# Two sequences' result stores moved to GpSimd's DMA queue, and every engine's order planned anew, in a one-core chunk-selected attention and squared-ReLU FFN kernel

## The chip, the cores and the metric

One core of a Trainium2 chip runs one program. The metric is the device time of an execution in microseconds; lower is better. Three runs of the kernel before took 264.72, 265.79 and 266.02 us, median 265.79 us.

## The reference

Four sequences of 768 tokens, 8 heads of 64. Keys are cut into 24 chunks of 32 tokens; for each query an upper bound of its score with each chunk is taken, and only the six best chunks are attended to, under a causal mask. The attention's output, 3072 rows of 512, goes through an FFN of width 2048 with a squared ReLU.

```python
ub = np.sum(np.maximum(q[:, :, :, None, :] * k_min[:, :, None, :, :],
                       q[:, :, :, None, :] * k_max[:, :, None, :, :]), axis=-1)
top_chunks = np.argsort(np.where(causal, ub, -1e9), axis=-1)[..., -top_k:]
scores = np.where(mask, scale * np.matmul(q, k.transpose(0, 1, 3, 2)), -1e9)
x = softmax(scores) @ v                      # 3072 x 512
return (np.maximum(x @ w_in, 0.0) ** 2) @ w_out
```

## The kernel before, in words

A sequence has six tiles of 128 queries. The first tile of each sequence needs no selection (all its chunks are among the six best), so the four first tiles are computed on their own at the start, and their FFN (input `x_first`, 4 tiles) is spread over the first sequence's attention. For the other five tiles of each sequence there are four pairs of heads, 16 pairs in all. Each pair has a **stage A** (`stage_a`): keys and queries are turned (`kT`, `qT`; by TensorE for sequences 0 and 1, by DMA transposes `kt`, `qt` on SP's queue for 2 and 3), VectorE reduces the chunks' largest and smallest keys (`kr`, L697), TensorE makes the bounds (`ub`, L660 and L662), VectorE sorts out the eight largest (`m`, L668), of which the sixth gives the selection (`selb`), which is turned (`sT`) and copied beside the queries (`qsc`) as extra rows, so that the score matmul itself adds the mask. **Stage B** (`stage_b`): scores in banks of 512 columns (`ps`, L782), exp on ScalarE (`e`, L804), the causal mask on VectorE (L759) or GpSimd (L762), values (`av`, L793), and VectorE's division into `x` (L612, L614). When a sequence's four pairs are done, its `x` is turned to `xT` (by TensorE for sequence 0, by five DMA transposes on SP's queue, L389, for 1, 2 and 3), and `ffn` follows: `up` (`ph`, L866), ReLU (`ht`, ScalarE L873 or VectorE L875), square (`h`, VectorE L884), `down` (`py`, L897), a copy to `ob` (L281 on ScalarE, L283 on VectorE), and the store of 256 KB, L910, on SP's queue. The FFN of sequence b is mixed with the attention of sequence b+1; that of the last runs alone at the end.

Nothing of this order is written out. Each piece of work is an `Op` of a `Plan`: the engines that may do it with an assumed cost each, a due time, what it needs, the buffers that it holds, and the DMA packets that it moves. `Plan.order` plays the program through: of the operations that could start on an engine within `wait` of the earliest, it takes the one that is due first, and for work that two engines may do, it takes the engine that could start it first. The instructions are then written in that order, so a due time or a cost that changes can change the order and the engine of all that comes later. Loads (`loads`) go through GpSimd's queue in a fixed sequence, at most eight at once; transposes, stores and the four first raw loads go through SP's queue. Each engine works off its queue in order: an instruction that waits holds up what stands behind it.

While TensorE waits in the first 26 us, `keep_warm` puts matmuls on a constant (`warm`, L539) in the gap, as many as the plan thinks fit (`op.fill`).

Buffers that matter here: `ps` 3, `ff` 2 (for `ph`, `py` and `xt`), `e` 6, `ob` 3. The constants' rows `kqc` for eight (slot, head) pairs are made once and copied seven times at the start (`kq_rows`), by whichever of GpSimd, VectorE and ScalarE the plan picks.

Of the kernel before, what the change touches and what calls it, by code (L numbers as in the profile page):

```python
# [13 lines left out]
ACT = mybir.ActivationFunctionType  # L14
# [66 lines left out]
class Plan:  # L81
# [18 lines left out]
        self.loads = []  # L100

    def op(self, where, due, fn, needs=(), tiles=(), packets=0, turns=False,
           late=0.0):
        op = Op(where, due, fn, [n for n in needs if n is not None],
                [t for t in tiles if t is not None], packets, turns)
        for t in op.tiles:
            t.users.append(op)
        op.late = late
        op.number = -1 if packets and not turns else len(self.ops) - len(self.loads)
        self.ops.append(op)  # L110
        if packets and not turns:
            self.loads.append(op)
        return op

    def order(self):
        free = {e: 0.7 for e in ("PE", "ACT", "DVE", "POOL", "SP")}
        slots = {tag: [(0.0, i) for i in range(n)] for tag, n in self.slots.items()}
        waiting = {}
        count = {}
        for op in self.ops:  # L120
            for t in op.tiles:
                t.left = len(t.users)
            count[op] = len(op.needs)
            for n in op.needs:
                waiting.setdefault(n, []).append(op)
        ready = [op for op in self.ops if not count[op]]
        landed, done = [], []
        dma = Transfers()
        while ready:
            found = []  # L130
            for op in ready:
                if op.packets and not op.turns and op is not self.loads[len(landed)]:
                    continue
                at = 0.0
                new = {}
                for t in op.tiles:
                    if not t.held:
                        new[t.tag] = new.get(t.tag, 0) + 1
                for tag, n in new.items():
                    at = max(at, sorted(slots[tag])[n - 1][0]  # L140
                             if n <= len(slots[tag]) else self.NEVER)
                if at == self.NEVER:
                    continue
                if op.packets and not op.turns and len(landed) >= 8:
                    at = max(at, landed[-8].end)
                for engine, cost in op.where.items():
                    st = max(at, free[engine])
                    for n in op.needs:
                        same = n.engine == engine and not n.packets
                        lag = (0.0 if engine == "PE" else self.BUSY) if same                             else self.HAND_OVER[n.engine]  # L150
                        st = max(st, n.end + lag)
                    for t in op.tiles:
                        if t.psum:
                            for e, end in t.last.items():
                                if e != engine and "PE" not in (e, engine):
                                    st = max(st, end + self.HAND_OVER[e])
                    found.append((st, op, engine, cost))
            assert found, "nothing can start"
            first = min(found, key=lambda f: (f[0], f[1].number))
            st, op, engine, cost = min(  # L160
                (f for f in found if f[2] == first[2] and f[0] <= first[0] + self.wait),
                key=lambda f: (round(f[1].due, 6), f[0], f[1].number))
            ready.remove(op)
            if engine == "PE":
                op.fill = 0
                fresh = [t for t in op.tiles if t.psum]
                if st < self.FILL and fresh and not any(t.held for t in fresh):
                    room = max([free[engine]] + [min(slots[t.tag])[0] for t in fresh])
                    op.fill = max(0, int((st - room - 0.3) / 0.216))
                if st < self.WARM:  # L170
                    cost *= 2
            op.engine, op.start, op.end = engine, st, st + cost
            free[engine] = op.end
            if op.packets:
                dma.add(op)
                if not op.turns:
                    landed.append(op)
            for t in op.tiles:
                if not t.held:
                    t.held = True  # L180
                    slot = min(slots[t.tag])
                    slots[t.tag].remove(slot)
                    t.slot = slot[1]
                t.last[engine] = max(t.last.get(engine, 0.0), op.end)
                t.left -= 1
                if not t.left:
                    slots[t.tag].append(
                        (max(u.end + self.HAND_OVER[u.engine] for u in t.users),
                         t.slot))
            for n in waiting.get(op, ()):  # L190
                count[n] -= 1
                if not count[n]:
                    ready.append(n)
            done.append(op)
        assert len(done) == len(self.ops), "operations left"
        return sorted(done, key=lambda op: op.start)
# [12 lines left out]
def kernel(  # L209
# [9 lines left out]
    nc = tc.nc  # L219
# [17 lines left out]
    QC = 128 * NS  # L237
    VW = 80
    NSET = 4
    P = dict(lead=[0, 207.45, 109.14, 153.29, -29.2, 112.12, 38.49, 53.35, 112.23, 30.95,  # L240
             26.44, 98.99, 127.21, 67.89, -1.38, 124.88], f_due=[452.52,
             -1393.33, -782.42, -326.54], sp='K0 Q0 K1 Q1', rows=[-2963.23,
             -1559.78, 780.78, -565.55, 1811.92, 457.36, -1818.66, -283.78],
# [3 lines left out]
             'q3 v2 v3 k3', shift={}, p0=-2735.84, wait=0.01, xt=(1, 2, 3),  # L247
             sel=2, loads='Q3 K3 V0 V1 Q2 K2 i0 V2 k0 V3 q0 i1 k1 v2 q1 i2 '
             'v0 i3 k2 q2 o1 o0 v1 o2 k3 o3 v3 q3')

    nc.scalar.preload_act_table_set("natural_log_exp_and_others")

# [13 lines left out]
    plan = Plan({"tp": 1, "ps": 3, "av": 2, "ff": 2, "e": 6, "h2": NFI + 6, "ht": 3,  # L266
                 "ob": 3, "kq": 6, "nt": 6,
                 "vn": B - 1, "x": 2, "xT": 2,
                 "st": 2, "kr": 2, "qp": 2, "qm": 2, "ubm": 2, "m8": 2, "rc": 2}, lambda *a: keep_warm(*a), P["wait"])
# [217 lines left out]
    made["rows", 0] = plan.op({"ACT": 0.88}, P["rows"][0], lambda e: kq_rows(e, 0),  # L487
                              [made["ident"]])
    for i in range(1, 2 * NSET):
        made["rows", i] = plan.op({"POOL": 0.80, "DVE": 0.40, "ACT": 0.75}, P["rows"][i],  # L490
                                  lambda e, i=i: kq_rows(e, i), [made["rows", 0]])
    made["tri"] = plan.op({"DVE": 0.15}, -900, lambda _: nc.vector.tensor_single_scalar(
        tri, ahead, 0.0, op=ALU.is_ge), [made["ahead"]])
# [326 lines left out]
                prev, [x], due + 7))  # L820


    def ffn(x, ready, rows, by_dma, due, rate, up_tags=("ff", "ff")):

        n = len(rows)
        xT = buffer("xT", [128, n, NKI, 128])
# [60 lines left out]
        def down(t, c0=0, c1=d_model):  # L887
            w = c1 - c0
            py = buffer("ff", [128, w], F32, name="py")
            ob = buffer("ob", [128, w], F32)  # L890
            op = None
            for part in range(NFI // 4):
                fs = range(4 * part, 4 * part + 4)

                def go(_, fs=fs):
                    for f in fs:
                        nc.tensor.matmul(py.tile,  # L897
                                         lhsT=h2[f][:, 128 * t:128 * (t + 1)],
                                         rhs=w_out_sb[:, f, c0:c1],
                                         start=(f == 0), stop=(f == NFI - 1))  # L900

                op = plan.op(
                    {"PE": 0.865 * w / d_model}, step(0.865 * w / d_model), go,
                    [op] + loaded["out", part] + [
                        o for f in fs for c0, c1, o in squared[f]
                        if c0 < 128 * (t + 1) and c1 > 128 * t],
                    [py] + [h2[f] for f in fs])
            op = plan.op({"ACT": 0.057 + w / 1200, "DVE": 0.075 + w / 960}, at[0] + 1,
                         lambda e: copy(e, ob.tile, py.tile), [op], [py, ob])
            plan.op({"SP": 0.35}, at[0] + 1, lambda _: nc.sync.dma_start(  # L910
                out[rows[t]:rows[t] + 128, c0:c1], ob.tile), [op], [ob],
                packets=2 * w, turns=True)

        return turn, up, down

# [21 lines left out]
    for b in range(B):  # L937
        x = buffer("x", [128, NS, d_model])
        x_done[b, 1] = []
        for p in range(NP * b, NP * (b + 1)):  # L940
# [3 lines left out]
        turn, up, down = ffn(  # L944
            x, lambda t, b=b: x_done[b, 1], [S * b + 128 * t for t in range(1, NT)],
            b in P["xt"], HALVES * NP * (b + 1) + P["due"][b], P["rate"][b],
            ("ps", "ps") if last else ("ff", "ff"))
        for c in range(2):
            tiles = range(2 * c, 2 + (NS - 2) * c)
            for t in tiles:  # L950
# [5 lines left out]
        if last:  # L956
            down(NS - 1, 0, 384)
            down(NS - 1, 384)
    computed = [op for op in plan.ops if op.turns or not op.packets]
    for i, change in P["shift"].items():  # L960
        computed[i].due += change
    with tc.manual_schedule():
        plan.write()

# [29 lines left out]
```

## Time and profile before

| what | value |
|---|---|
| median of three runs | 265.79 us (264.72 to 266.02) |
| profiled execution, first to last instruction (span) | 263.6 us |
| around the span, if that execution took the median | 2.2 us |
| TensorE busy, share of the span | 251.4 us, 95% |
| VectorE, ScalarE, GpSimd busy | 183.0, 197.8, 106.4 us |
| granted TensorE clock, mean | 0.994 |

The profile is one execution seen by the hardware profiler. Its rows name the line of the kernel, the engine (PE is TensorE's matmuls, PEld its weight loads, DVE VectorE, ACT ScalarE, POOL GpSimd, SP SyncE; a q behind the name is the engine's queue), what is written and read, how many there are, their busy time and the mean ns of one, and the engine's idle time ahead of them with what ended it. Times within the span count from its start. The page with the time in 40 slices gives busy tenths.

### The profile page before, as it was taken

To read this page: it belongs to the slowest core of one execution; us is meant where nothing else is said; L and a number is where in the kernel's file an instruction comes from. 1 tells how busy PE (TensorE), PEld (TensorE's weight loads), DVE (VectorE), ACT (ScalarE), POOL (GpSimd) and SP (SyncE) were. 2 spreads that over 40 slices of the span, in tenths; PEclk is the share of its full clock that TensorE was granted. 3 is DMA by queue.
4 is the path that set the end of the run, shared out by engine and by line. 5 is a ranking of instruction groups with operands and counts; after the bars stand their busy time and mean duration, and the time that the engine had idled before them with its cause. 6 is when DMAs were issued, how large, how long until landed. Compare 5 with 4: busy or idle time off the path is not lost.

```text
span 263.6 us, 6555 instructions
## 1 busy us (share of the span) xinstructions
PE 251.4 (95%) x2382; PEld 164.1 (62%) x2405; DVE 183.0 (69%) x663; ACT 197.8 (75%) x395; POOL 106.4 (40%) x185
## 2 busy tenths in 40 slices
PE   6899999999999999999999999998999999999995
PEld 1577566666687666665686645666865564765443
DVE  7569999778999999998999943644757142455000
ACT  6658897859899999999989845987866692677111
POOL 7998987799555599833311201110200010000000
PEclk9799999999999999999999999999999999999999
DMA  8999999999999999995440001154000113400122
GB/s 153 156 175 180 181 198 190 94 126 174 170 151 166 149 157 143 123 145 148 87 93 15 2 20 75 44 82 101 2 0 15 42 44 99 120 2 0 40 82 80
DMA packets 106336, 26.51 MB, mean 101 GB/s; under 512 B 99008, under 2 KB 103360, under 8 KB 106304
## 3 DMA queue, kind: packets, MB, share of 16 engines
q0 software_dynamic: 75088, 13.11, 67.9%
q1 hardware_dynamic: 31216, 12.98, 24.0%
q8 instruction: 19, 0.31, 0.5%
q14 instruction: 13, 0.11, 0.2%
HBM read 27.26 MB, written 6.29 MB: 127 GB/s over the span
## 4 chain that ended last, share of the span: by engine, by line
PE 62%; DVE 24%; ACT 8%; issue 3%; DMA 2%; SPq 0%; ACTq 0%; DVEq 0%
PE py L897 25%; PE ph L866 20%; PE ps L782 8%; PE av L793 4%; DVE h L884 4%; DVE kr L697 4%; DVE m L668 3%; DVE qsc L283 3%; ACT e L804 2%; DMA xT<-x 2%; ACT ht L873 2%; DVE x L614 2%; ACT qsc L281 2%; DVE kqc L283 1%; DVE ubm L722 1%
## 5 line engine op out<-in xcount | busy, mean ns | idle before, releaser
L866 PE MATMUL ph<-xT,w_in_sb 128*128 128x256 bf16 (+2 forms) x592 | 95.7, 304 | 1.6 <-DMA xT<-x 1.2
L804 ACT ACTIVATE e<-ps 128x512 bf16<-128x512 f32 x160 | 86.4, 608 | 7.5 <-PE ps L782 4.4
L897 PE MATMUL py<-w_out_sb,h 128*128 128x512 bf16 (+2 forms) x377 | 87.9, 370 | 1.2
L762 POOL TENSOR_SCALAR_AFFINE_SELECT e<-e 128x128 bf16<-128x128 bf16 (+1 forms) x88 | 31.0, 365 | 101.0 <-ACT e L804 89.1
L866 PEld LDWEIGHTS <-w_in_sb 128*128 128x128 bf16 x592 | 55.6, 97 | 24.9 <-DMA xT<-x 1.6
L873 ACT ACTIVATE ht<-ph 128x384 bf16<-128x384 f32 (+2 forms) x130 | 58.9, 457 | 16.2 <-PE ph L866 12.5
L884 DVE TENSOR_TENSOR h<-ht 128x256 bf16<-128x256 bf16 (+2 forms) x148 | 47.8, 333 | 16.4 <-ACT ht L873 12.9
L897 PEld LDWEIGHTS <-h 128*128 128x128 bf16 x400 | 36.2, 97 | 33.8
L782 PE MATMUL ps<-qsc,kqc 88*128 88x128 bf16 (+1 forms) x320 | 51.7, 272 | 0.3 <-DVE ubm L722 0.2
L782 PEld LDWEIGHTS <-kqc 88*128 88x128 bf16 x320 | 27.6, 97 | 14.8 <-issue 0.8
L281 ACT COPY ob<-py 128x512 f32<-128x512 f32 (+2 forms) x22 | 12.5, 570 | 29.2 <-PE py L897 29.1
L793 PEld LDWEIGHTS <-e 128*128 128x128 bf16 x640 | 29.6, 97 | 6.4 <-issue 0.3
L793 PE MATMUL av<-vn,e 128*128 128x65 bf16 x480 | 29.6, 193 | 0.0
L759 DVE TENSOR_TENSOR e<-e,tri 128x128 bf16<-128x128 bf16 (+1 forms) x40 | 9.7, 242 | 14.9 <-ACT e L804 14.2
L614 DVE TENSOR_TENSOR x<-av,rc 128x320 bf16<-128x320 f32 (+1 forms) x40 | 18.7, 472 | 0.5
L668 DVE MAX8 m<-ubm 128x8 f32<-128x24 f32 x160 | 15.5, 167 | 0.0
L697 DVE TENSOR_REDUCE kr<-kT 128x24 bf16<-128x768 bf16 x16 | 14.8, 951 | 0.2
L697 DVE TENSOR_REDUCE kr<-kt 128x24 bf16<-128x768 bf16 x16 | 14.8, 935 | 0.0
L793 PE MATMUL av<-v,e 128*128 128x65 bf16 x160 | 13.9, 193 | 0.1
L875 DVE TENSOR_SCALAR ht<-ph 128x256 bf16<-128x256 f32 (+2 forms) x18 | 8.2, 454 | 8.2 <-PE ph L866 8.2
L612 DVE RECIPROCAL rc<-av 128x5 f32<-128x5 f32 (+1 forms) x40 | 7.2, 184 | 9.4 <-PE av L793 8.5
L281 ACT COPY qsc<-sT 24x256 bf16<-24x256 bf16 (+1 forms) x29 | 12.4, 427 | 1.6 <-DMA sT<-selb 0.9
(92 smaller groups left out, 258.7 us busy)
## 6 DMA issues: line engine op xcount, KB each, us to landing
out_dram<-ob SPq DMA_DIRECT2D x23, 256.0 KB, 2.2
w_in_sb<-in_moe_w_in_dram POOLq DMA_DIRECT2D x4, 512.0 KB, 7.2
w_out_sb<-in_moe_w_out_dram POOLq DMA_DIRECT2D x4, 512.0 KB, 8.8
vn<-in_v_dram POOLq DMA_DIRECT2D x15, 128.0 KB, 6.9
nt<-in_k_dram POOLq DMA_DIRECT2D x10, 128.0 KB, 6.6
nt<-in_q_dram POOLq DMA_DIRECT2D x10, 128.0 KB, 5.3
kn<-in_k_dram POOLq DMA_DIRECT2D x8, 80.0 KB, 7.0
qn<-in_q_dram POOLq DMA_DIRECT2D x8, 80.0 KB, 5.7
```

Source lines behind the costliest of these rows:

```text
L281: nc.scalar.copy(dst, src)
L614: return plan.op({"DVE": 0.06 + 0.00108 * D * n}, due, lambda _: nc.vector.tensor_mul(x(), av[:, :, 0:D], rc[:, 0:n].unsqueeze(2).to_broad ...
L668: nc.vector.max(out=m8[:, i, hh], in_=ubm[:, i, hh])
L697: nc.vector.tensor_reduce(kr[:, mm].rearrange("d (t c) -> d t c", c=128 // CH) if b >= BY_DMA else kr[:, mm], part(kT).rearrange("d t (c j ...
L762: nc.gpsimd.affine_select(out=e, in_=e, compare_op=ALU.is_ge, fill=0.0, base=0, channel_multiplier=-1, pattern=[[0, n], [1, 128]])
L782: nc.tensor.matmul(ps[:, 128 * c:128 * (c + nt)], lhsT=kqs[:, s, hh, 128 * j:128 * (j + 1)], rhs=qss[:, s, hh, 128 * (t0 - 1):128 * (t0 - ...
L793: nc.tensor.matmul(av[:, t - 1], lhsT=e[:, 128 * c:128 * (c + 1)], rhs=value_tile(b, h, j), start=(i == 0 and c == 0), stop=(i == len(BANK ...
L804: nc.scalar.activation(e.tile, ps.tile, ACT.Exp, scale=scale), [sc], [ps, e])
L866: nc.tensor.matmul(ph.tile, lhsT=w_in_sb[:, ki, 128 * f:128 * (f + 1)], rhs=xT[:, c0 // 128:c1 // 128, ki], start=(ki == 0), stop=(ki == N ...
L873: nc.scalar.activation(ht.tile, ph.tile, ACT.Relu)
L884: {"DVE": 0.067 + w / 1920}, at[0] + P["h2"], lambda _: nc.vector.tensor_mul(h2[f][:, c0:c1], ht.tile, ht.tile), [op], [ht, h2[f]])))
L897: nc.tensor.matmul(py.tile, lhsT=h2[f][:, 128 * t:128 * (t + 1)], rhs=w_out_sb[:, f, c0:c1], start=(f == 0), stop=(f == NFI - 1))
```

## The change

1. The five stores of each of sequences 1 and 2 (`out=(1, 2)`, ten of the 25) are issued from GpSimd's queue and not from SP's. To the plan such a store costs GpSimd 0.80 us where it cost SP 0.35; a new mark `free` keeps it out of the fixed sequence of loads.
2. 247 entries `moves` each add a number to the due times of a stretch of operations; `order` gives the 85 loads a new sequence; `wait` goes from 0.01 to 0.00818.
3. The plan's cost of a copy of the constant rows on VectorE goes from 0.40 to 0.80 us.

Arithmetic, tiles and buffers stay as they are. All line numbers of the changed kernel from L100 on are larger, by 77 in the stages (L897 is L974, L389 is L466).

```diff
     def op(self, where, due, fn, needs=(), tiles=(), packets=0, turns=False,
-           late=0.0):
+           late=0.0, free=False):
...
-        op.number = -1 if packets and not turns else len(self.ops) - len(self.loads)
+        op.load = bool(packets) and not turns and not free
+        op.number = -1 if op.load else len(self.ops) - len(self.loads)
...
-                if op.packets and not op.turns and op is not self.loads[len(landed)]:
+                if op.load and op is not self.loads[loads]:
...
+    P.update(moves=[(1308, 1386, 42.49), (1355, 1356, 68.64), (1177, 1180, -47.7),
...
+             order=[0, 3, 4, 1, 2, 5, 6, 10, 9, 8, 7,
...
+             wait=0.00818)
...
-        made["rows", i] = plan.op({"POOL": 0.80, "DVE": 0.40, "ACT": 0.75}, P["rows"][i],
+        made["rows", i] = plan.op({"POOL": 0.80, "DVE": 0.80, "ACT": 0.75}, P["rows"][i],
...
-            plan.op({"SP": 0.35}, at[0] + 1, lambda _: nc.sync.dma_start(
-                out[rows[t]:rows[t] + 128, c0:c1], ob.tile), [op], [ob],
-                packets=2 * w, turns=True)
+            plan.op({"POOL": 0.80} if by_pool else {"SP": 0.35}, at[0] + 1, lambda e: (
+                nc.gpsimd if e == "POOL" else nc.sync).dma_start(
+                    out[rows[t]:rows[t] + 128, c0:c1], ob.tile), [op], [ob],
+                packets=2 * w, turns=not by_pool, free=by_pool)
...
+    for i0, i1, change in P["moves"]:
+        for op in computed[i0:i1]:
+            op.due += change
+    if P["order"]:
+        plan.loads = [plan.loads[i] for i in P["order"]]
```

What the two builds' instructions show of it: TensorE 2399 matmuls for 2405 (six `warm` ones fewer); SP 13 stores for 23 of 256 KB; GpSimd 10 stores more. Work that either of two engines may do lies otherwise in part, as the prediction counts it.

More of the change, by code (lines that the diff above doesn't have):

```diff
@@ L108, in op @@
         op.late = late
-        op.number = -1 if packets and not turns else len(self.ops) - len(self.loads)
+        op.load = bool(packets) and not turns and not free
+        op.number = -1 if op.load else len(self.ops) - len(self.loads)
         self.ops.append(op)
-        if packets and not turns:
+        if op.load:
             self.loads.append(op)
@@ L126, in order @@
         ready = [op for op in self.ops if not count[op]]
-        landed, done = [], []
+        landed, done, loads = [], [], 0
         dma = Transfers()
@@ L177, in order @@
                     landed.append(op)
+                    loads += op.load
             for t in op.tiles:
@@ L239 @@
     NSET = 4
-    P = dict(lead=[0, 207.45, 109.14, 153.29, -29.2, 112.12, 38.49, 53.35, 112.23, 30.95,
+    P = dict(out=(1, 2), moves=[], order=[], lead=[0, 207.45, 109.14, 153.29, -29.2, 112.12, 38.49, 53.35, 112.23, 30.95,
              26.44, 98.99, 127.21, 67.89, -1.38, 124.88], f_due=[452.52,
@@ L249 @@
              'v0 i3 k2 q2 o1 o0 v1 o2 k3 o3 v3 q3')
+    P.update(moves=[(1308, 1386, 42.49), (1355, 1356, 68.64), (1177, 1180, -47.7),
[67 rows of a table added]
+             5.95), (1053, 1057, 1.94)], order=[0, 3, 4, 1, 2, 5, 6, 10, 9, 8, 7,
[5 rows of a table added]
+             wait=0.00818)
     nc.scalar.preload_act_table_set("natural_log_exp_and_others")
@@ L820, in stage_b, with ffn @@
                 prev, [x], due + 7))
-    def ffn(x, ready, rows, by_dma, due, rate, up_tags=("ff", "ff")):
+    def ffn(x, ready, rows, by_dma, due, rate, up_tags=("ff", "ff"), by_pool=False):
         n = len(rows)
@@ L946 @@
             b in P["xt"], HALVES * NP * (b + 1) + P["due"][b], P["rate"][b],
-            ("ps", "ps") if last else ("ff", "ff"))
+            ("ps", "ps") if last else ("ff", "ff"), b in P["out"])
         for c in range(2):
@@ L958 @@
             down(NS - 1, 384)
-    computed = [op for op in plan.ops if op.turns or not op.packets]
+    computed = [op for op in plan.ops if not op.load]
     for i, change in P["shift"].items():
         computed[i].due += change
+    for i0, i1, change in P["moves"]:
[3 more added lines that the diff above has]
+        plan.loads = [plan.loads[i] for i in P["order"]]
     with tc.manual_schedule():
```

72 rows, old and new, of the table sel are left out of this document.

## The prediction

> **What bounds the kernel now.** I read the page's totals, TensorE's waits, the chain of waits, and then the timeline where a wait stands. Sequences are counted from 0.
>
> ```profile
> span 263.6 us, 6555 instructions
> PE 251.4 (95%) x2382; PEld 164.1 (62%) x2405; DVE 183.0 (69%) x663; ACT 197.8 (75%) x395; POOL 106.4 (40%) x185
> PE ph L866 <- DMA xT<-x: 1.2, 1, 1.2
> PE xt L286 <- ACT kqc L281: 0.5, 1, 0.5
> ```
>
> TensorE is busy for 95% of the span, and of its waits after the start only one is over 0.5 us: 1.2 us for the turned `xT` of sequence 2's FFN. So no engine's queue has much to give back; the change can win a few waits or make some. But from 75 to 135 us VectorE and ScalarE are nearly full as well:
>
> ```profile
> 75.00:90.00 15.00, 14.89 (x171) 11.28 (x171) 14.85 (x57) 14.23 (x31) 8.82 (x14) 1.00 1.87 149
> 90.00:105.00 15.00, 14.33 (x145) 9.45 (x145) 14.84 (x53) 14.21 (x30) 14.24 (x21) 1.00 2.25 155
> 105.00:120.00 15.00, 14.70 (x168) 9.30 (x169) 14.82 (x61) 14.78 (x29) 8.88 (x20) 1.00 1.44 132
> 120.00:135.00 15.00, 14.88 (x166) 10.57 (x166) 13.74 (x56) 13.72 (x29) 3.89 (x12) 1.00 0.51 120
> ```
>
> (After the width: busy us of PE, PEld, DVE, ACT, POOL; granted clock; DMA share; GB/s.) Between 75 and 120 us VectorE idles 0.5 us of 45. Work that the new plan moves onto VectorE there is paid for at full price.
>
> I work against the span of 263.6 us; the median of the three runs, 265.8, lies 2.2 us above it, and I add these 2.2 to every result.
>
> **The change, part by part.**
>
> *The start.* The chain of the first 17 us goes through VectorE:
>
> ```profile
> 0.81 0.46 SPq L399 DMA_DIRECT2D raw<-in_k_dram  x1
> 4.33 0.69 DVE L283 COPY kqc<-kqc 24x768 bf16<-24x768 bf16 x1
> 5.30 0.62 DVE L283 COPY kqc<-kqc 24x768 bf16<-24x768 bf16 x1
> 5.96 0.91 DVE L283 CAST k<-raw 128x512 bf16<-128x512 f32 x1
> 6.92 0.40 PE L286 MATMUL T<-ident,k 128*128 128x128 bf16 x4 [1.78 <-DVE k L283]
> raw<-in_k_dram SPq DMA_DIRECT2D x2, 256.0 KB, 4.0
> 15.74 1.70 PE L539 MATMUL ph<-warm 128*128 128x256 bf16 x14
> 9.39 0.79 POOL L461 DMA_DIRECT2D w_in_sb<-in_moe_w_in_dram  x1
> w_in_sb<-in_moe_w_in_dram POOLq DMA_DIRECT2D x4, 512.0 KB, 7.2
> ```
>
> The first raw tile lands at about 0.81 + 4.0 = 4.8 us, but its cast starts at 5.96, behind a third copy of the constant rows. In the changed order VectorE has two of these copies and ScalarE the other, and the small memset between them is GpSimd's. The cast can start at 4.33 + 0.69 = 5.0, and TensorE's first transpose comes 0.9 us sooner. Later in the start, the changed order has six `warm` matmuls fewer ahead of the first `ph`: 6 x 1.70 / 14 = 0.7 us. Together up to 1.6 us, but the first `ph` needs the first block of `w_in`, which lands at about 9.39 + 7.2 = 16.6, and its issue moves back by the GpSimd memset. After the `warm` ones, `ph` started at 15.74 + 1.70 = 17.44. So 0.6 to 0.8 us can be had here, and no more. A little later comes a second cap:
>
> ```profile
> 13.59 1.79 POOL L454 DMA_DIRECT2D qn<-in_q_dram  x2
> qn<-in_q_dram POOLq DMA_DIRECT2D x8, 80.0 KB, 5.7
> 20.52 0.44 PE L286 MATMUL qT<-ident,qn 128*128 128x128 bf16 x5
> 21.43 1.39 ACT L281 COPY qsc<-qT 64x640 bf16<-64x640 bf16 x2
> ```
>
> The second `qn` is issued at about 14.5 and lands at 20.2; the turning of queries can hardly move. But the copies behind it began at 21.43 only because ScalarE was still on `kqc`; they can begin at about 20.2 + 0.44 + 0.1 = 20.7. That keeps 0.7 us. From there to 30 us the order on all engines is the same as before. Value **-0.6 us**; bounds -1.6 (no cap holds) and 0 (the loads take it all).
>
> *The wait for `xT`.*
>
> ```profile
> 174.20 7.91 SPq L389 DMA_TRANSPOSE xT<-x  x5
> 175.44 5.17 DMA xT<-x
> 180.65 0.61 PE L866 MATMUL ph<-xT,w_in_sb 128*128 128x256 bf16 x4 [1.16 <-DMA xT<-x]
> DMA to landing us min/median/max: 2.4/2.5/5.2
> 172.86 0.12 PE av L793 x4
> 172.98 0.86 PE py L897 x4
> 173.84 0.67 PE ps L782 x6
> ```
>
> The second transpose took 5.17 us from issue to landing, against a median of 2.5, and the matmuls on it waited 1.2 us. Between the last `av` of sequence 2 and this `ph` the order before has four groups of four `py`, nine `ps` banks and 36 `av`; the changed order has five, eleven and 28. By the chain's rows (0.86 us for four `py`, 0.67 for six `ps` matmuls, which are three banks, 0.12 for four `av`) that is 0.86 + 0.45 - 0.24 = 1.1 us more work in front of it. So even a second transpose that is as late costs only 0.1 us, and one at the median costs nothing. Value **-1.1 us**; bounds -1.2 and 0 (it is later still). For the FFN of sequence 1 the same count is equal before and after, and for that of sequence 3 it grows, so I put nothing there. But if a transpose of sequence 1 should be 2.7 us over the median, up to +0.7 us: its cover is no thicker than the one that failed here.
>
> *The stores.* Taking ten off SP saves its queue ten issues of 0.33 us. On GpSimd a DMA issue keeps the engine:
>
> ```profile
> L910 SPq DMA_DIRECT2D out_dram<-ob x25: 332/333/531, 54.2 to 260.8; - x25
> out_dram<-ob SPq DMA_DIRECT2D x23, 256.0 KB, 2.2
> L447 POOL DMA_DIRECT2D vn<-in_v_dram x15 | 13.4, 924 | 0.0
> w_out_sb<-in_moe_w_out_dram POOLq DMA_DIRECT2D x4, 512.0 KB, 8.8
> 150.00:165.00 15.00, 14.90 (x114) 8.24 (x115) 7.32 (x32) 8.30 (x17) 0.70 (x2) 1.00 0.12 42
> L762 POOL TENSOR_SCALAR_AFFINE_SELECT e<-e 128x128 bf16<-128x128 bf16 x68 | 22.7, 346 | 88.8 <-ACT e L804 79.0 <-DVE x L614 9.6
> L804 ACT ACTIVATE e<-ps 128x512 bf16<-128x512 f32 x160 | 86.4, 608 | 7.5 <-PE ps L782 4.4 <-PE av L793 2.0 <-POOL e L762 0.4
> ```
>
> Ten issues of about 0.92 us are 9 us of GpSimd, in a stretch where it is busy 0.7 us of 15. They hurt only through the masks queued behind a store: the store waits for `ob`, holds GpSimd 0.92 us, and a mask behind it (0.35 us) is late for its `av`. In the changed order eight of the ten have no mask behind them that TensorE needs within 3 us of work after its scores. The two others, one in each sequence, have 2.0 and 2.1 us of TensorE work between scores and `av`; scores to masked tile take about 1.3 us (an estimate: exp 0.6, mask 0.35, two hand-overs), so 0.7 us are spare against one issue of 0.92. Value **0**; bounds 0 and +0.9 (one issue in full). The landing grows from 2.2 us to somewhere between 2.2 and the 8.8 of the slowest GpSimd row; with three `ob` and a `down` every 3.4 us (16 matmuls at 0.215) even 8.8 is under the 10 us until a buffer is wanted again.
>
> The Trainium skill (SBUF — State Buffer, section "SBUF: two separate sides", the warning on SWDGE) speaks against the move: a DMA issued from GpSimd needs descriptors that GpSimd cannot write while VectorE holds the shared port pair. By that a store could land late and its issue stretch; the GpSimd issues of 75 to 120 us, with VectorE full, took 0.9 us all the same, so it changes neither value.
>
> *All other order.* The assignment of work that two engines share moves between VectorE and ScalarE:
>
> ```profile
> L875 DVE TENSOR_SCALAR ht<-ph 128x256 bf16<-128x256 f32 x15 | 6.3, 419 | 8.2 <-PE ph L866 8.2
> L875 DVE TENSOR_SCALAR ht<-ph 128x384 bf16<-128x384 f32 x1 | 0.6, 551 | 0.0
> L283 DVE COPY qsc<-qT 64x640 bf16<-64x640 bf16 x10 | 4.8, 482 | 0.1
> L283 DVE COPY kqc<-kT 64x768 bf16<-64x768 bf16 x6 | 3.3, 550 | 1.9 <-PE kT L286 1.8
> L759 DVE TENSOR_TENSOR e<-e,tri 128x256 bf16<-128x256 bf16 x12 | 3.4, 285 | 1.3 <-ACT e L804 1.0
> ```
>
> VectorE gets ten more ReLUs, 5 x 0.42 + 5 x 0.55 = 4.9 us, and loses two `qsc`, two `kqc` and three masks, 0.96 + 1.10 + 0.86 = 2.9 us; the single copies that change sides besides (one of constant rows off it; an `ob`, an `xT`, a cast onto it) come to about +1. So VectorE carries +3 us and ScalarE about as much less. Where it lies decides: six `qsc` copies leave VectorE in the fullest stretch, and about six of the ReLUs come in from 120 us on, where VectorE has 1.3 us in 15 to spare by the row of 120 to 135. The distances in TensorE work that the orders leave are mixed: from scores to the `av` of a masked tile the shortest falls from 1.6 to 1.4 us (1.3 are needed), while the middle distance at which a `ps` bank is used again grows from 1.8 to 2.1 us, and from a pair's bounds to its first scores the shortest grows from 3.9 to 4.5 us. Value **0**, between -3 (the other waits, and the gaps that they hide, go too) and +3 (VectorE's added work in full).
>
> Sum: -0.6 - 1.1 + 0 + 0 = -1.7 us: 261.9 us of span, **264.1 us** of time.
>
> **The rivals.**
>
> *The order gives back what it wins* (25%). Another transpose is late where the cover is thin, or a masked tile at 1.4 us waits behind a busy ScalarE: a span of 263.6, 265.8 us. For it: a transpose has been late by 2.7 us with nothing in the kernel's order that explains it, and the new plan has several tight distances. Against it: the cover at the one wait that counts has grown. The Trainium skill (Runtime: NRT & Kernel Launch, instruction fetch mechanics) says that instructions stream in by DMA in blocks of 16 KiB, 256 instructions. By that a refill recurs whatever the order, and meets another transfer when the order shifts; no view here names the transfer that it meets.
>
> *VectorE sets the pace* (20%), the slower side. If the +3 us fall where VectorE is full, 75 to 150 us, each costs TensorE the same: -0.6 - 1.1 + 3.1 = +1.4 with all else kept, +2.1 with a late transpose at sequence 1: 267.2 to 267.9 us, say 267.5. It decides once VectorE's idle time from 120 us on (1.3 us by 135) is used up. Against it: six `qsc` copies leave that engine.
>
> *The small waits go as well* (13%): about 3 us more off, 261.0 us. For it: the distances that grew.
>
> *The stores don't matter* holds in my forecast already: they are worth 0 by themselves, and the change's gain would be the same with them on SP.
>
> **How the numbers follow.** Forecast 42%: 264.1, its own spread 262.8 to 265.4. A measurement of this kernel can tell about 0.5%, 1.3 us, from no change: "faster" is below 264.5, "slower" above 267.1. Faster: 27 points of the forecast, 13 of the small waits, 4 of the give-back = 0.44. Slower: 18 of VectorE, 3 of the give-back = 0.21. Within: 0.35. The range takes the forecast, the give-back and most of VectorE's case: 261.6 to 267.4.
>
> **What would show it.** Start: first `ph` at about 16.8 us, not 17.4. `xT`: TensorE's wait for `DMA xT<-x` under 0.3 us. Stores: no wait of `av` on GpSimd's masks, GpSimd busy some 10 us more. Order: VectorE's row at 186 us, ScalarE's at 194. I am wrong if TensorE shows new waits on `e`, `h` or `ub` of more than 1 us together between 75 and 150 us, or if the start's gain is gone by 30 us.

## The result, and the profile after

The changed kernel takes 264.73 us (median of 20 runs, 263.53 to 266.19), the kernel before, on the same chips, 265.99 us (20 runs, 264.72 to 267.73). The ratio is 0.995, with a 95% interval of 0.9931 to 0.9969: a gain of 1.3 us, where 1.7 were forecast. The profiled execution has a span of 262.4 us and took 264.36 us.

The totals of the changed kernel's page, its GpSimd row of stores, and all of TensorE's waits from 30 us to the end:

```profile
span 262.4 us, 6547 instructions
PE 253.6 (97%) x2399; PEld 164.0 (62%) x2399; DVE 185.9 (71%) x669; ACT 195.5 (75%) x385; POOL 113.8 (43%) x199
L988 POOL DMA_DIRECT2D out_dram<-ob x10 | 5.6, 558 | 22.0 <-ACT ob L358 21.4
```

```profile
PE xt L363 <- ACT ob L358: 0.3, 1, 0.3
PE sT L363 <- DVE selb L804: 0.2, 1, 0.2
PE ph L943 <- DVE ht L952: 0.2, 1, 0.2
```

The wait for `xT` is gone, and behind the start no wait of TensorE is over 0.3 us. (TensorE's busy row can't be compared with that of the first trace of before, which lacks 23 `py` records; a second trace of before, with all of them, has 253.9 us.) VectorE carries 185.9 us, 186 were forecast; ScalarE 195.5 (194). GpSimd gained 7.4 us and not 10: a store's issue holds it 0.56 us, not the 0.92 of a load.

The transposes of sequence 2 (instructions on `xT` from 170 to 184 us), and what TensorE did ahead of the first `ph`:

```profile
L943 PE MATMUL ph<-xT,w_in_sb x23: 269/272/274, 178.1 to 183.9; 128*128 128x256 bf16 x23
L466 SPq DMA_TRANSPOSE xT<-x x5: 1190/1257/1967, 171.5 to 176.7; - x5
DMA to landing us min/median/max: 2.4/2.5/4.4
```

From the first issue (171.5) to the first `ph` (178.1) are 6.6 us; before there were 6.45 (174.20 to 180.65), the wait of 1.2 among them. Two transposes are late here as well, but they are the fourth (4.1 us from issue to landing) and the fifth (4.4), which TensorE needs later.

The start, on TensorE and on GpSimd. These two fences are timelines of the changed kernel; the one behind them is GpSimd's of a second trace of the kernel before:

```profile
5.50 0.40 PE L363 MATMUL T<-ident,q 128*128 128x128 bf16 x4 [0.91 <-DVE q L360]
17.25 1.05 PE L943 MATMUL ph<-xT,w_in_sb 128*128 128x256 bf16 x8 [0.24 <-DMA w_in_sb<-in_moe_w_in_dram]
21.22 0.44 PE L363 MATMUL qT<-ident,qn 128*128 128x128 bf16 x5 [0.34 <-DMA qn<-in_q_dram]
23.74 1.03 PE L943 MATMUL ph<-xT,w_in_sb 128*128 128x256 bf16 x8 [0.33 <-ACT xT L358]
```

```profile
3.95 0.37 POOL L499 MEMSET vn<- 128x40 bf16 x1
4.01 1.20 POOL L446 DMA_DIRECT2D q<-in_q_dram  x1
5.21 1.04 POOL L446 DMA_DIRECT2D v<-in_v_dram  x1
9.69 0.80 POOL L538 DMA_DIRECT2D w_in_sb<-in_moe_w_in_dram  x1
```

```profile
3.85 1.01 POOL L369 DMA_DIRECT2D q<-in_q_dram  x1
4.86 0.89 POOL L369 DMA_DIRECT2D k<-in_k_dram  x1
9.40 0.79 POOL L461 DMA_DIRECT2D w_in_sb<-in_moe_w_in_dram  x1
```

TensorE's first transpose comes at 5.5 us and not at 6.9, as forecast and more. But a memset stands ahead of the loads, the second of them is issued 0.35 us later and that of `w_in` at 9.7 and not 9.4, its first block lands at 17.2 us, and the `ph` on it waits for it. The gain is used up there: `qT` and the second row of `ph` come 0.7 and 0.3 us later than in the first trace of before. (TensorE's granted clock was half of full from 7.3 to 14.1 us in this trace, and from 8.6 to 12.0 in the first trace of before; what the first `ph` waits for is the load all the same.)

The end, which the prediction did not look at. SP's semaphore instructions behind the landing of the last store, first before (262.3 to 262.78 us), then changed (261.45 to 261.57):

```profile
L989 SPq EVENT_SEMAPHORE  x7: 27/28/28, 262.4 to 262.7; - x7
```

```profile
L1072 SPq EVENT_SEMAPHORE  x1: 28/28/28, 261.5 to 261.5; - x1
```

At the end SP goes through nine semaphore waits in a fixed order; the last eight of them are for the eight semaphores that its DMAs signal in turn. Before, the wait for the last store (landed 262.35) is the third, followed by six more, whose transfers had long landed, at 0.061 us each; in the changed kernel it is the last of the row. The shutdown of all engines starts behind them, 0.37 us sooner.

### The profile page after: what moved, and what is told of

The parts are those of the page before. It is cut to its first block, busy times and chain, and to the rows that moved or that the text cites. A ratio compares the mean times of both kernels' runs of the same rounds, so it can differ in the third digit from the quotient of the medians.

```text
span 262.4 us, 6547 instructions
## 1 busy us (share of the span) xinstructions
PE 253.6 (97%) x2399; PEld 164.0 (62%) x2399; DVE 185.9 (71%) x669; ACT 195.5 (75%) x385; POOL 113.8 (43%) x199
## 4 chain that ended last, share of the span: by engine, by line
PE 66%; DVE 19%; POOL 6%; ACT 3%; DMA 2%; issue 1%; DVEq 0%; ACTq 0%; POOLq 0%
PE py L974 28%; PE ph L943 21%; PE ps L859 10%; PE av L870 6%; DVE h L961 4%; DVE kr L774 4%; DMA qn<-in_q_dram 2%; DVE m L745 2%; DVE ht L952 2%; DVE qsc L360 2%; POOL v L446 1%; DVE qp L790 1%; POOL kn L524 1%; DVE ubm L799 1%; DVE qm L790 1%
## 5 line engine op out<-in xcount | busy, mean ns | idle before, releaser
L943 PE MATMUL ph<-xT,w_in_sb 128*128 128x256 bf16 (+2 forms) x592 | 96.7, 304 | 0.9 <-ACT xT L358 0.3
L974 PE MATMUL py<-w_out_sb,h 128*128 128x512 bf16 (+2 forms) x400 | 91.3, 370 | 0.0
L839 POOL TENSOR_SCALAR_AFFINE_SELECT e<-e 128x128 bf16<-128x128 bf16 (+1 forms) x91 | 32.4, 363 | 85.2 <-ACT e L881 79.6
L950 ACT ACTIVATE ht<-ph 128x384 bf16<-128x384 f32 (+2 forms) x120 | 54.7, 456 | 16.2 <-PE ph L943 11.7
L974 PEld LDWEIGHTS <-h 128*128 128x128 bf16 x400 | 36.2, 97 | 33.8
L859 PE MATMUL ps<-qsc,kqc 88*128 88x128 bf16 (+1 forms) x320 | 52.7, 272 | 0.0
L870 PE MATMUL av<-vn,e 128*128 128x65 bf16 x480 | 31.2, 193 | 0.1
L952 DVE TENSOR_SCALAR ht<-ph 128x256 bf16<-128x256 f32 (+2 forms) x28 | 12.9, 465 | 12.5 <-PE ph L943 12.4
L988 POOL DMA_DIRECT2D out_dram<-ob x10 | 5.6, 558 | 22.0 <-ACT ob L358 21.4
L836 DVE TENSOR_TENSOR e<-e,tri 128x128 bf16<-128x128 bf16 (+1 forms) x37 | 8.5, 237 | 8.6 <-ACT e L881 7.8
L524 POOL DMA_DIRECT2D vn<-in_v_dram x15 | 13.5, 903 | 0.4 <-issue 0.4
```

Source lines behind the costliest of these rows:

```text
L839: nc.gpsimd.affine_select(out=e, in_=e, compare_op=ALU.is_ge, fill=0.0, base=0, channel_multiplier=-1, pattern=[[0, n], [1, 128]])
L859: nc.tensor.matmul(ps[:, 128 * c:128 * (c + nt)], lhsT=kqs[:, s, hh, 128 * j:128 * (j + 1)], rhs=qss[:, s, hh, 128 * (t0 - 1):128 * (t0 - ...
L870: nc.tensor.matmul(av[:, t - 1], lhsT=e[:, 128 * c:128 * (c + 1)], rhs=value_tile(b, h, j), start=(i == 0 and c == 0), stop=(i == len(BANK ...
L943: nc.tensor.matmul(ph.tile, lhsT=w_in_sb[:, ki, 128 * f:128 * (f + 1)], rhs=xT[:, c0 // 128:c1 // 128, ki], start=(ki == 0), stop=(ki == N ...
L950: nc.scalar.activation(ht.tile, ph.tile, ACT.Relu)
L952: nc.vector.tensor_scalar_max(ht.tile, ph.tile, 0.0)
```

## The experiments

Fourteen traces, of twelve runs and the two kernels, are read with one table. "First scores" is the start of the first `ps` of pair 0: up to there the operations are the same set in all kernels, matmuls on constants apart. From there on every kernel has the same matmuls, so the third column differs by waits alone. The fourth is from the end of the last matmul to the end of the span, the fifth TensorE's gap ahead of the first `ph` on sequence 2's `xT`. All in us, worked out from the start and end of TensorE's records. The gap is counted from the start of the matmul ahead of it, less the 0.22 us that such a step takes without a wait, and is 0.16 us more than in a row of waits.

| kernel | start, order, stores | first scores | from there to the last matmul | last matmul to end | gap at `xT` |
|---|---|---|---|---|---|
| before | old, old, SP | 29.42 | 230.98 | 3.24 | 1.3 |
| before_again | old, old, SP | 30.05 | 230.30 | 3.23 | 0.8 |
| before_pad8 | old, old, SP | 30.32 | 230.02 | 3.23 | 0.3 |
| before_pad52 | old, old, SP | 29.64 | 230.75 | 3.22 | 0 |
| before_stores_pool | old, old, GpSimd | 30.20 | 230.32 | 2.87 | 0.8 |
| before_new_start | new, old, SP | 30.39 | 231.78 | 3.40 | 0.3 |
| early_new | old, new to 117 us, SP | 29.99 | 230.34 | 3.22 | 1.0 |
| late_new | old, new from 117 us, GpSimd | 29.26 | 231.16 | 2.86 | 0 |
| after | new, new, GpSimd | 29.69 | 229.86 | 2.85 | 0 |
| after_pad25 | new, new, GpSimd | 30.73 | 229.89 | 2.86 | 0 |
| after_stores_sp | new, new, SP | 30.87 | 229.77 | 3.51 | 0 |
| after_old_start | old, new, GpSimd | 31.23 | 229.58 | 2.87 | 0 |
| after_old_start_2 | old, new, GpSimd | 29.98 | 229.59 | 2.85 | 0 |
| after_old_start_sp | old, new, SP | 30.92 | 229.70 | 3.23 | 0 |

**The stores alone.** Two runs take the queue of the ten stores by itself, with everything else of the program in place:

```diff
 # after_stores_sp, on the changed kernel (the plan still counts them to GpSimd)
-            plan.op({"POOL": 0.80} if by_pool else {"SP": 0.35}, at[0] + 1, lambda e: (
-                nc.gpsimd if e == "POOL" else nc.sync).dma_start(
+            plan.op({"POOL": 0.80} if by_pool else {"SP": 0.35}, at[0] + 1, lambda _: (
+                nc.sync).dma_start(
 # before_stores_pool, on the kernel before (by_pool for sequences 1 and 2)
-            plan.op({"SP": 0.35}, at[0] + 1, lambda _: nc.sync.dma_start(
+            plan.op({"SP": 0.35}, at[0] + 1, lambda _: (nc.gpsimd if by_pool else nc.sync).dma_start(
```

> The changed kernel with its plan, its orders and its choice of engines kept, only that the ten stores are issued from SP's queue at the same places of the program. My theory: the stores are worth 0, the time stays at the changed kernel's 264.7 us (0.995 of before), GpSimd loses the ten store issues (5.6 us), and TensorE shows no wait for xT. Rival A, that the stores on GpSimd's queue are what took the wait for xT away (a store ahead of the transposes on SP's queue makes one late): 1.0 us or more come back, 265.7 to 266.0 us, with a TensorE wait for xT of about 1 us at sequence 2's FFN.

> The kernel before with its plan and orders kept, only that the ten stores of sequences 1 and 2 are issued from GpSimd's queue at the same places. My theory: worth 0, 266.0 us (1.000 of before, within 0.3%), and the 1.2 us wait for xT at 180 us stands. Rival A (the store on SP's queue ahead of the transposes makes one late): that wait goes, 264.8 us. Rival B (GpSimd's masks queue behind the stores): TensorE waits for masked tiles, up to 0.6 us for each store that has a mask right behind it, 266.5 us or more.

Measured: 264.89 us (ratio 0.9977, 0.995 to 1.0005) with the stores back on SP; 265.31 (0.9981, 0.9946 to 1.0016) with the old order and the stores on GpSimd. Rival A falls: with the stores on GpSimd the old order still waits for `xT`, and the changed order does not with them on SP. Rival B falls: no wait for a masked tile shows. TensorE's waits of before_stores_pool:

```profile
PE T L286 <- DVE k L283: 1.8, 1, 1.8
PE wt L539 <- DVE warm L351: 1.1, 1, 1.1
PE ph L866 <- DMA xT<-x: 0.6, 1, 0.6
```

Neither interval tells 0.2% from nothing, but the fourth column does: in the eight traces with all stores on SP it is 3.22 to 3.51 us, in the six with ten of them on GpSimd 2.85 to 2.87. SP's last waits in before_stores_pool (262.4 to 262.55 us) and in after_old_start_sp (262.5 to 263.0 us) are one and seven:

```profile
L989 SPq EVENT_SEMAPHORE  x1: 28/28/28, 262.5 to 262.5; - x1
```

```profile
L1126 SPq EVENT_SEMAPHORE  x7: 28/28/28, 262.6 to 263.0; - x7
```

So the stores are worth 0.37 us, at the very end. The traces show why: in all fourteen, SP's DMAs signal the eight semaphores strictly in turn. With the ten stores SP has 74 DMAs, and the last signals the second of the eight; without them it has 64, and the last signals the eighth, whose wait is the last. By this it is the number of DMAs left on SP that counts; no run here has another number than these two.

**The refill of TensorE's instructions.** The page of the kernel before lists, among its DMA queues, one for instructions; its 19 packets of 16 KB are TensorE's, one for every 256 instructions or so (2405 matmuls and as many weight loads make 253 for each):

```profile
q8 instruction: 19, 0.31, 0.5%
```

One of them starts at 176.84 us, in the middle of the late transpose. The Trainium skill (Runtime: NRT & Kernel Launch, section "Instruction fetch mechanics") says that instructions come by DMA in blocks of 16 KiB; the trace agrees for this queue, 0.31 MB in 19 packets; a second queue for instructions, q14, moves 8 KB in a packet. The test moves the refills by a few instructions more in TensorE's idle time of the start:

```diff
+    def pad(n):
+        for _ in range(n):
+            nc.tensor.matmul(wt[0][:, 0, 0:1], lhsT=warm, rhs=warm[:, 0:1], start=True, stop=True)
...
             op.fn(op.engine)
+            if op.engine == "PE":
+                turn += 1
+                if turn == 2:          # 4 in after_pad25
+                    self.pad(52)       # 8 in before_pad8, 25 in after_pad25
```

> The kernel before with 52 one-column matmuls on a constant put in the idle time that TensorE has from 5.1 to 6.9 us; nothing else is changed, and nothing of the result depends on them. Each is two instructions more (weights and matmul), so every later refill of TensorE's instructions, a 16 KB transfer that the packets of the trace show at 176.84 us in the middle of the second transpose, comes 104 instructions, some 5 us, sooner: about 171.5 us, ahead of the transposes of sequence 2 (174.2 on). Theory of the refill: no transpose of sequence 2 takes 5.2 us, the wait of 1.2 us for xT goes, and the time is 264.8 us (0.9955). Rival, that the second transpose is late by its place in the order (the store ahead of it, the stages beside it): the wait stays and the time is 266.0 us.

> The control of the run with 52: eight of these one-column matmuls, 16 instructions, which moves the refills by about 0.8 us, to 176.0, still inside the second transpose of sequence 2 (issued at 175.44, landed at 180.6). Theory of the refill: a transpose of sequence 2 still takes over 4 us, the wait for xT stays between 0.5 and 1.5 us, 266.0 us. Rival, that matmuls at the start by themselves shorten the run (a warmer clock, or a shifted start): it gains as much as the run with 52.

> The kernel before once more, for a second trace of it. If the wait for xT at 180 us is fixed in its order it is there again at 0.5 us or more; if it hangs on when the refill of TensorE's instructions meets a transpose, its length differs from 1.2 us by over 0.3. The first ph of the first trace, at 17.3 us, is earlier here or later by how the first loads land: within 0.2 us if my reading of the start holds, by 0.5 us or more if the landings scatter.

> The changed kernel with 25 one-column matmuls on a constant in TensorE's idle time from 6.2 to 7.4 us, 50 instructions, so that the refill of 176.5 us comes some 2.5 us sooner, at about 174, inside the second transpose of sequence 2 (issued at 172.8). My step said that the thicker cover (1.1 us more TensorE work ahead of the matmuls on xT) is what removes the wait: the second transpose takes over 4 us and the wait stays under 0.4 us, time 264.7 us. Rival, that the changed kernel lost the wait only because the refill meets the fourth transpose and not the second: a wait of 0.8 to 1.3 us for xT, 265.7 us.

Measured, with the start of the refill from the trace's packets. Instructions on `xT`, 170 to 184 us, of before_pad52, before_pad8, before_again and after_pad25:

```profile
L394 SPq DMA_TRANSPOSE xT<-x x5: 1188/1265/1268, 175.5 to 180.7; - x5
DMA to landing us min/median/max: 2.4/2.5/3.1
```

```profile
L394 SPq DMA_TRANSPOSE xT<-x x5: 1195/1265/1812, 175.2 to 180.9; - x5
DMA to landing us min/median/max: 2.5/2.7/4.1
```

```profile
  DMA xT<-x: 0.6, 1
DMA to landing us min/median/max: 2.4/2.5/4.6
```

```profile
L471 SPq DMA_TRANSPOSE xT<-x x5: 1190/1267/2217, 172.6 to 178.7; - x5
DMA to landing us min/median/max: 2.4/3.3/4.2
```

With 52 the refill starts at 172.1, ahead of the transposes: none is late (3.1 us at most), the wait is gone. With 8 it starts at 176.1 and two are late (3.6 and 4.1 us); in the second trace of before at 177.3, and two take 4.6 and 4.0. A packet of q14 comes too, at 177.9 to 179.2 in these three and the first trace of before; in before_pad52 it meets a transpose without the refill, and 3.1 us is what that one took. So the refill makes the transposes late, and how late varies: the gap at `xT` was 1.3, 0.8, 0.8, 0.3 and 0.3 us in five old orders whose refill met them. In after_pad25 the refill (176.0) meets the second and third transposes of the changed order; the second lands at 178.0 us, and the first `ph` starts at 179.2, without a wait. So it is the thicker cover that protects the changed order, and not only a luckier place of the refill: my reading stands, the rival falls. The test is a mild one: the second transpose took 4.15 us here, and one of 4.1 us costs the old order 0.3 (before_pad8). One of 5.17 us, as in the first trace of before, would have landed at 179.0, still ahead of the `ph`; that is worked out, and no run shows it.

The times say something else: 265.76 us (1.0007, 0.9977 to 1.0037) with 52 and 265.63 (0.9999, 0.9964 to 1.0034) with 8. Taking this one wait from the old order gains nothing that can be measured; the interval leaves room for 0.6 us. Its trace shows a likely reason. Two of TensorE's waits in it stand in no row of the first trace, one for a load at 65 us, one for a masked tile at 86 us:

```profile
PE qT L291 <- DMA qn<-in_q_dram: 0.8, 2, 0.6
PE av L808 <- POOL e L777: 0.3, 1, 0.3
```

The refills come elsewhere now, and the loads land otherwise; the third column is 230.75 us, within what the old order takes with the wait. That the moved refills themselves make these two waits is not shown. after_pad25 takes 264.52 us (0.9954, 0.9936 to 0.9973), the same as the changed kernel.

**The start, exchanged.** The first 173 operations, up to 27.9 us, are the same set in both plans; each kernel gets the other's order and engines for them:

```diff
     def write(self):
-        for op in self.order():
+        order = self.order()
+        head = []
+        for i, engine, fill in self.HEAD:       # 173 entries of the other kernel's plan
+            op = self.ops[i]
+            op.engine, op.fill = engine, fill
+            head.append(op)
+        first = set(head)
+        order = head + [op for op in order if op not in first]
...
+        for op in order:
```

> The kernel before, only that its first 173 operations (all that starts in the first 27.9 us, the same set in both kernels) come in the changed kernel's order and on its engines, warm matmuls included. In 35 runs the span of the kernel before lay between 261.9 and 266.2 us (standard deviation 1.1), that of the changed one in 20 runs between 261.8 and 264.5 (0.6). If the change's gain is that of the start (the slow runs have another start, or a third window at half clock): 264.7 us and a spread near 0.6. If it is that of the order behind 28 us: 265.8 us and a spread near 1.1. By my prediction's step the start would be worth 0.6 us: 265.2.

> The reverse: the changed kernel with the first 173 operations in the order and on the engines of the kernel before. If the gain is that of the start: 265.8 us, spread 1.1. If it is that of the order behind 28 us: 264.7 us, spread 0.6. By my prediction's step the start would be worth 0.6 us: 265.3.

Measured: the kernel before with the new start 266.37 us, ratio 1.0037 (1.0007 to 1.0068), slower than before; the changed kernel with the old start 264.15 us, 0.994 (0.9919 to 0.9962). The gain is that of the order behind 28 us with its stores, and in front of the old order the new start costs 0.9 us by the medians of this comparison (266.37 against 265.51). Not all of that lies in the start: in the one trace of before_new_start the third column is 1.3 us above the mean of the other five old orders, with waits of 0.5 us for a masked tile at 86 us and for a ReLU at 142 us. In before_new_start GpSimd's memset comes first again and TensorE waits for the loads (its timeline and its waits):

```profile
3.95 0.37 POOL L476 MEMSET vn<- 128x40 bf16 x1
9.78 0.77 POOL L515 DMA_DIRECT2D w_in_sb<-in_moe_w_in_dram  x1
```

```profile
PE qT L340 <- DMA qn<-in_q_dram: 1.1, 2, 0.9
PE ph L920 <- DMA w_in_sb<-in_moe_w_in_dram: 0.3, 1, 0.3
```

The first scores of the ten traces with the old start come at 29.3 to 31.2 us, mean 30.1; of the four with the new one at 29.7 to 30.9, mean 30.4, a difference within their scatter. The first trace of before, from which I worked, was the second earliest of all: its `w_in` landed at 16.1 us, in the others at 16.6 to 18.2.

**The order behind the start, cut at 117 us.** The same edit with longer lists: 968 operations (the old start and the new order behind it) ahead of the old order, and 973 of the old ahead of the new.

> The kernel before, only that its operations from the 174th to the 968th (27.9 to about 117 us) come in the changed kernel's order and on its engines; the start and all that follows stay as before, the ten stores on SP's queue too. Theory 1, that the gain of the order behind the start is spread: of the 1.5 us that the changed order with the old start is below the kernel before, this stretch brings about half, 265.0 us. Theory 2, that the gain is the wait for xT at 180 us alone: nothing here, 265.6 us. Theory 3, that VectorE's added work costs something in its full stretch: 266 us or more.

> The complement: the first 973 operations (to about 117 us) as in the kernel before, the rest in the changed kernel's order and on its engines, the ten stores on GpSimd's queue. Theory 1 (spread gain): about half of the 1.5 us, 265.0 us. Theory 2 (the wait for xT is all): the whole, 264.2 us. In both the matmuls on sequence 2's xT do not wait.

Measured: early_new 264.99 us (0.9987, 0.9956 to 1.0018); late_new 266.21 (1.003, 1.0001 to 1.0059). The cut does not tell the theories apart. In late_new the two plans don't fit at the seam: TensorE waits there, at 121.8 us, for an exp that the one has put late and the other expects early (its waits):

```profile
PE ps L1086 <- ACT e L1108: 0.9, 1, 0.9
```

That is a wait of the experiment. early_new does not come out slower, so VectorE's added work before 117 us costs nothing that shows (theory 3 falls); it keeps the wait for `xT`, 1.0 us in its trace. Between theories 1 and 2 the run is inconclusive.

**The better version.** The changed kernel with the old start once more, and beside it the same with the stores on SP:

> The changed kernel with the start of the kernel before, once more, as the version that beats both: 264.2 us, 0.994 of before, if the first seven runs were typical.

> The same with the ten stores issued from SP's queue, beside it on the same chip. If the stores are worth 0: the same 264.2 us within 0.4. If GpSimd's queue is worth something by itself: 264.6 us or more.

Measured: 264.31 us (0.9966, 0.9944 to 0.9989) and 265.39 (1.0004, 0.9981 to 1.0028). With 264.15 in the run before, the changed order with the old start is faster than the kernel before. That it beats the changed kernel too is not shown: by the medians it is ahead by 0.4 to 0.6 us, but against the kernel before in the same comparison it has 0.994 and 0.9966, and the order with the changed start 0.995 and 0.9954. The stores make 1.1 us between these two, more than the 0.37 that the end shows; all three pairs have that sign (0.2, 0.4 and 1.1 us by the medians). The granted clocks account for most of the rest: five of the twelve runs with the stores on SP had a mean clock of 0.98, and three of the twelve with them on GpSimd. Among the others, all at 0.992 or more, the means differ by 0.5 us, with a standard error of 0.2.

## Why the prediction was right, and where it was not

The direction held, the gain is 0.5% where 0.64% were forecast (1.7 of 265.8), and 264.7 us lies within the range, 0.6 over the forecast. But the sum came out well because errors of its terms cancel.

- **The start: forecast -0.6, and wrong.** The step that failed is "0.6 to 0.8 us can be had here": the cap by the first block of `w_in` was worked out from one trace, as 16.6 by its row's median (in that trace the block landed at 16.1), and the issue "moves back by the GpSimd memset" was left without a size. It moved back 0.3 us, the landings scatter by 2 us, and TensorE waits for them. The first scores came at 29.7 us, against 29.4 in the first trace of before, so the forecast's own sign, "if the start's gain is gone by 30 us", speaks against this part. What the new start costs is less sure: in front of the changed order the medians give 0.2 to 0.6 us (264.5 and 264.7 against 264.2 and 264.3), the ratios to before nothing, the traces' first scores 0.3; in front of the old order it is the 0.9, in part behind the start. I put it at 0 to +0.3.
- **The wait for `xT`: forecast -1.1; mechanism right, size off.** No trace of the changed order waits there, with the refill in the transposes (after_pad25) too. But 1.2 us (1.3 in the table) was the worst of what the old order does: its gaps were 1.3, 0.8, 0.8, 0.3, 0.3 and, with the refill out of the way, 0. The mean is 0.6.
- **The stores: forecast 0, with bounds 0 and +0.9; it is -0.37.** No mask is late, as said. What I never asked is who waits for a store at the end of the program.
- **All other order: forecast 0.** From the first scores to the last matmul the six old orders took 230.0 to 231.8 us (mean 230.7), the six changed ones 229.6 to 229.9 (mean 229.7). Of the 1.0 us, 0.6 is `xT`. The other 0.4 is no steady gain: less their gap at `xT`, four of the six old orders lie at 229.5 to 229.7, like the changed ones, and only before_pad52 and before_new_start lie 1.0 and 1.8 higher, by other waits that come and go. VectorE's 3 us more cost nothing; they lie where it has room.

The sum by these: 0.3 - 0.6 - 0.4 = -0.7 at the least and 0 - 0.6 - 0.4 - 0.4 = -1.4 at the most, beside the measured -1.3 (by the interval -0.8 to -1.8).

The granted clock is a term that neither sum has. Of the runs with a clock on record, those of kernels with the old start fall into two groups, at 0.981 or less and at 0.986 or more (last section). With the first group left out on both sides, the mean time lies below that of before in the same comparison by 0.9, 0.9 and 1.1 us in the runs with the changed order and the stores on GpSimd (after_old_start_2, after_pad25, after_old_start), by 0.4 in both with the changed order and the stores on SP, and by 0.6 in before_stores_pool, each with a standard error of 0.2 to 0.3. So at like clocks the order is worth about 0.4 us and the stores about 0.5. That the changed kernel has no run of the first group would add some 0.3 us; for the 20 runs of before in the result the clocks are not on record, so this last share stays an estimate.

Of the rivals, "the order gives back what it wins" was right in part, by the start and not by a transpose: the late transposes of sequence 1 (up to 4.5 us in the changed kernel) made no wait. VectorE did not set the pace.

## What to carry to other kernels

A wait that stands in one trace is one draw: before it is priced, look whether something that moves from run to run (the landing of a load, a refill) makes it, and price it at less than it shows. An order that keeps more work between a transfer and its use is worth more than the one wait that it removes, since it holds when the transfer is late; taking the one cause away gained nothing that twelve runs could tell. Where medians differ by less than 1 us, look at the clock that each run was granted before the difference is put down to the change. At the start, ask first what stands ahead of the first load on its queue, and at the end, what the last engine still waits for.

## What the runs showed of the hardware

- In 13 of the 14 traces a refill of TensorE's instructions (16 KB, about every 256 instructions) falls into the five transposes of sequence 2: two of them take 3.3 to 5.2 us instead of 2.5, and SP's issue of one takes 1.8 to 2.7 us instead of 1.26. In the 14th, before_pad52, it comes ahead of them, and none takes over 3.1. In sequence 3 a transpose issued 0.1 us after the start of a refill landed after the usual 2.5 us (after_old_start_sp), so not every meeting does it.
- At the end SP works off a fixed row of nine waits, 0.061 us each where the transfer landed long ago. Its DMAs signal eight semaphores in turn; the last store's place in the row was worth 0.37 us.
- A store of 256 KB holds GpSimd for 0.56 us, a load there 0.92. The changed kernel's ten stores landed 2.3 to 3.2 us after their issue, the three with VectorE idle meanwhile (2.3 to 3.0) hardly sooner than the seven with VectorE busy for 0.6 of the time or more (2.3 to 3.2).
- The mean granted TensorE clock was 0.981 or less in 38 of 184 runs of kernels with the old start and in none of 56 with the new one. In the kernel before, such runs have spans of 265.2 us on the mean, the others 263.3. No trace of such a run was kept; in the six traces with means of 0.987 to 0.994 the clock is half of full for 6.8 us (0.987) or 3.4 us (0.994), beginning 7.3 to 9.2 us into the span. For the mean over many runs this speaks for the new start, by some 0.4 us (38 of 184 times 1.9).
